# One visit instead of two for the attention's products with v, with two column groups in banks of the first layer's pool

## The chip, the core and the metric

The kernel runs on one core of a Trainium2 chip. Its engines have queues of their own: TensorE (PE, matrix products; PEld is its weight load), VectorE (DVE), ScalarE (ACT), GpSimd (POOL, here the issuer of loads) and SyncE (SP, here the issuer of stores and of transposing transfers). The metric is the device time of one execution, in microseconds. PE writes its results to PSUM, which has eight banks of 512 float32 per partition.

## What is computed

Attention within chunks of 64 rows, then a two-layer network on its output, cut from the reference:

```python
# q, k, v: (8, 8, 576, 64); chunks of 64 rows of the sequence
scores = scale * np.matmul(q_c, k_c.transpose(0, 1, 2, 4, 3))
scores = scores - np.max(scores, axis=-1, keepdims=True)
attn = np.exp(scores)
attn = attn / (np.sum(attn, axis=-1, keepdims=True) + 1e-09)
out = np.matmul(attn, v_c)
# x: (4608, 512) = out with its 8 heads side by side; w_in (512, 2048), w_out (2048, 512)
h = x @ w_in
g = h * (1.0 / (1.0 + np.exp(-beta * h)))
return g @ w_out
```

## The kernel before

The 4608 rows are cut into 18 **units** of 256 rows (four chunks for each of eight heads), and units are paired into nine **blocks** of 512 rows. A unit's attention has five steps. `emit_T` brings q and k into transposed form (from unit 8 on by transposing transfers on SP). `emit_sc` multiplies them: 32 small matmuls (64x64 tiles of the array) into a PSUM tile of two banks, and ACT takes the exponential of it into `et`. `emit_pv` multiplies `et` with v. A column of constants stands beside the 64 columns of v, so that each of the products has 65 columns, the last of which is the sum for the norm. `emit_norm` (DVE) takes the reciprocal of these sums and multiplies, into `x16`. From unit 6 on `emit_xt_dma` (SP) then writes `x16` transposed into `xt`, the first layer's input.

A unit has two **halves** `s` of 128 rows; one half is eight column groups (four `g` for each of two row halves `r` of the array, each `r` with a PSUM bank of its own), and each group is written by two matmuls, one for each 64 partitions `c`. So a half is 16 matmuls.

The first layer of block j (`emit_m`, 16 groups m) is four matmuls of 512 columns into one bank `hps`, then tanh on ACT (`sg`, L326), then the **gate** on DVE (L306), which reads `hps` and `sg` and writes `gt`. The second layer is done with seven products of half size (`emit_prod`, each in two parts t of eight matmuls of 256 columns, L434) on sums of parts of `gt` (`emit_sum`, DVE, L378) and of the weights; their results are gathered in the banks `ya` and `yb`, from which ACT copies or DVE adds (L454) them out, and SP stores them.

PSUM from block 3 on: `ps_p`, a ring of four banks, for the `hps` tiles; `ps_s`, one tile of two banks, for a unit's scores and then for its products with v, first one half, then the other; `ya` and `yb`. A tile of a ring is given out when the readers of its last content are done. Before block 3 a pool `ps_x` has two banks in the place of `ya` and `yb`, and units below 8 put one half there and the other half in `ps_s`, with all 32 matmuls in one visit of PE. A **visit** is a run of such small matmuls between two groups of full size.

The order on every engine is the order in which the program is written: nothing reorders it. In block j the main loop makes a list of items for the first layer of block j, the products of block j-1 and the attention of units 2j+2 and 2j+3, each with a place between 0 and 1, and emits them sorted by place (and by priority, the second number, where places are equal). For a unit from 8 on, with `a0` its start and `w` = 0.43 its share of the block:

```python
return [(a0, 2, ("sc", u)), (a0 + 0.34 * w, 3, ("pv", u, 0)),
        (a0 + 0.35 * w, 3, ("norm", u, 0)), (a0 + 0.60 * w, 3, ("pv", u, 1)),
        (a0 + 0.61 * w, 3, ("norm", u, 1)), (a0 + 0.10 * w, 3, ("T", u + 1))]
```

Units 8 to 17 are worked on in blocks 3 to 7, two in each. The first unit of a block starts at 0.03, the second at 0.46.

Of the kernel before, what the change touches and what calls it, by code (L numbers as in the profile page):

```python
# [8 lines left out]
FP32 = mybir.dt.float32  # L9
FP16 = mybir.dt.float16  # L10
ACTF = mybir.ActivationFunctionType
ALU = mybir.AluOpType
# [3 lines left out]
def kernel(  # L16
# [10 lines left out]
    nc = tc.nc  # L27
    B, H, S, D = q.shape
# [9 lines left out]
    NV = 16  # L38
# [8 lines left out]
    rd_p = ctx.enter_context(tc.tile_pool(name="rd", bufs=2))  # L47
    x_p = ctx.enter_context(tc.tile_pool(name="x16", bufs=4))
# [5 lines left out]
    ps_p = ctx.enter_context(tc.tile_pool(name="ps_p", bufs=4, space=bass.MemoryType.PSUM))  # L54
    ps_s = ctx.enter_context(tc.tile_pool(name="ps_s", bufs=1, space=bass.MemoryType.PSUM))
    ps_x_open = tc.tile_pool(name="ps_x", bufs=1, space=bass.MemoryType.PSUM)
    ps_x = ps_x_open.__enter__()
# [12 lines left out]
    vbig = big.tile([128, NV, H, VP], FP16)  # L70
# [5 lines left out]
    XU = 8  # L76
# [91 lines left out]
    x_t = {}  # L168
    x16_t = {}
# [68 lines left out]

    def emit_pv(u, halves=(0, 1)):
        et = et_t[u]  # L240
        for s in halves:
            i = 2 * u + s
            pool, tag = (ps_x, "x") if s == 0 and u < XU else (ps_s, "s")
            x = pool.tile([128, 2, 4, 128], FP32, tag=tag, name="x")
            for g in range(4):
                for r in range(2):
                    for c in range(2):
                        nc.tensor.matmul(  # L248
                            out=x[64 * c:64 * c + 64, r, g, 0:D + 1],
                            lhsT=(et[64 * r:64 * r + 64, s, 4 * c + g, :] if u < XU else  # L250
                                  et[64 * r:64 * r + 64, g % 2, 4 * s + 2 * c + g // 2, :]),
                            rhs=vbig[64 * r:64 * r + 64, i % NV, 4 * c + g, 0:D + 1],
                        )
            x_t[u, s] = x

    def emit_norm(u, s):
        x = x_t.pop((u, s))
        rd = rd_p.tile([128, 2, 4, 1], FP32, tag="rd", name="rd")
        nc.vector.reciprocal(out=rd, in_=x[:, :, :, D:D + 1])
        x16 = x_p.tile([128, 2, 4, D], FP16, tag="x16", name="x16")  # L260
        for r in ([0, 1] if u < 2 else [slice(0, 2)]):
            o = x16[:, r]
            nc.vector.tensor_tensor(  # L263
                out=o, in0=x[:, r, :, 0:D], in1=rd[:, r].to_broadcast(list(o.shape)), op=ALU.mult
            )
        x16_t[u, s] = x16
# [196 lines left out]
    with tc.manual_schedule():  # L463
# [3 lines left out]
        for a, eng, dst in ((0, nc.sync, raw0), (1, nc.gpsimd, qk0[1])):  # L467
            for i, src in enumerate((q, k)):
                eng.dma_start(
                    out=dst[i],  # L470
                    in_=src[0, HH * a:HH * a + HH, 0:UNIT, :].rearrange("h (p r) d -> p h r d", r=2),
# [27 lines left out]
        loads_to(4)  # L499
        emit_idle(8, 128)  # L500
        emit_pv(0)
        emit_norm(0, 0)
        emit_norm(0, 1)
        emit_idle(12, 128)
        emit_xt_pe(0, 0)
# [4 lines left out]
        emit_m(0, 0, 0, 256)  # L510
        emit_m(0, 1, 0, 256)
        emit_pv(1)
        emit_norm(1, 0)
        emit_norm(1, 1)
        emit_m(0, 2, 0, 256)
# [9 lines left out]
        for s in range(4):  # L525
            for t in range(4):
                if s == 2 and t == 1:
                    emit_T(2)
                    for i in (0, 2, 1, 3):
                        emit_wt(i, (0,))  # L530
                    emit_wt(0, (1,))
                if s == 2 and t == 2:
                    emit_sc(2)
                if s == 3 and t == 0:
                    emit_pv(2)
                    emit_norm(2, 0)
                    emit_norm(2, 1)
                    emit_T(3)
                if s == 3 and t == 3:
                    emit_xt_unit(2)  # L540
                emit_t(0, t, 4 * s, 4 * s + 4)
# [16 lines left out]

        def att_items(u, a0, w):
            if u >= XU:  # L560
                return [(a0, 2, ("sc", u)), (a0 + 0.34 * w, 3, ("pv", u, 0)),
                        (a0 + 0.35 * w, 3, ("norm", u, 0)), (a0 + 0.60 * w, 3, ("pv", u, 1)),
                        (a0 + 0.61 * w, 3, ("norm", u, 1)), (a0 + 0.10 * w, 3, ("T", u + 1))]
            return [(a0, 2, ("sc", u)), (a0 + 0.40 * w, 3, ("pv", u)),
                    (a0 + 0.41 * w, 3, ("norm", u, 0)), (a0 + 0.55 * w, 3, ("norm", u, 1)),
                    (a0 + (0.70 if u + 1 < XU else 0.10) * w, 3, ("T", u + 1))]

        for j in range(1, NB):
# [4 lines left out]
            if j == 1:  # L573
                items += [(0.04 * m, 0, ("h", m)) for m in range(8)]
                items += [(0.32 + 0.085 * (m - 8), 0, ("m", m)) for m in range(8, KFF)]
                items += [(0.30, 3, ("T", 4)), (0.52, 2, ("sc", 4)), (0.70, 2, ("pv", 4)), (0.71, 3, ("norm", 4, 0)),
                          (0.80, 3, ("norm", 4, 1)), (0.56, 3, ("Th", 5, "kT")), (0.63, 3, ("Th", 5, "qT"))]
                items += [(c, 3, ("wt", i)) for i, c in ((1, 0.47),)]
            else:
                m0 = 0.36 if j == 2 else 0.02  # L580
                items += [(m0 + (1 - m0) * m / KFF, 0, ("m", m)) for m in range(KFF)]
                for i, p in enumerate((1, 2, 6, 5, 7, 3, 4)):
                    for t in range(2):
                        items.append((0.98 * (2 * i + t) / 14, 1, ("prod", p, t)))
                if j == NB - 1:
                    for i, c in ((2, 0.74), (0, 0.82), (1, 0.86), (3, 0.90)):
                        items.append((c, 4, ("pre", i)))
                for i in range(4):
                    s0 = (0.01, 0.08, 0.25, 0.33)[i] if j == 2 else 0.005 + 0.07 * i
                    items.append((s0, 4, ("sum", i)))  # L590
                if j == 2:
                    items += [(c, 3, ("wt", i)) for i, c in ((2, 0.36), (3, 0.55))]
                    items += [(0.03, 0, ("sc", 5)), (0.06, 2, ("xp", 4, 0)), (0.09, 2, ("xp", 4, 1)),
                              (0.17, 2, ("pv", 5)), (0.18, 3, ("norm", 5, 0)), (0.19, 3, ("norm", 5, 1)),
                              (0.24, 3, ("T", 6)), (0.30, 2, ("xp", 5, 0)), (0.32, 2, ("xp", 5, 1))]
                if j + 1 < NB:
                    if j == 2:
                        items += att_items(6, 0.36, 0.27) + att_items(7, 0.60, 0.27)
                    else:
                        for i in range(2):  # L600
                            items += att_items(2 * j + 2 + i, 0.03 + 0.43 * i, 0.43)
# [64 lines left out]
```

## Time and profile before

| What | Value |
|---|---|
| Three timed runs | 282.84, 284.44, 285.32 us |
| The profiled execution's own time | 282.25 us |
| Its span, first to last instruction | 280.5 us |
| PE busy | 270.0 us (96%) |
| DVE busy | 194.4 us (69%) |
| ACT busy | 147.6 us (53%) |
| One block, from one to the next product behind the first unit's scores (155.57 to 183.99 us) | 28.42 us |
| of it DVE busy | 20.18 us |
| PE's granted clock in every stretch | 1.00 |

The page cuts the span into 40 slices; a digit is the busy share of an engine in tenths. A line of the timeline has the start, the length of a run of equal instructions, engine, line, operation, what it writes from what, shape and count; in brackets stands the idle time before it and what ended that. Matmuls overlap, so a group's length is longer than what it costs: the cost is read from start to start. The same holds on DVE, where the end of one instruction lies beside the start of the next. A line of the view of waits has who waited for whom, the total in us, the number of waits and the longest.

### The profile page before, as it was taken

The numbers are of one execution on the slowest core, as the hardware profiler recorded it, in microseconds if no ns is written. First come the engines' busy times: TensorE is split into PE (matmuls) and PEld (weight loads), VectorE is DVE, ScalarE is ACT, GpSimd is POOL, SyncE is SP. The second block draws the span as 40 slices with busy tenths as digits, with TensorE's granted clock in tenths as the row PEclk, the third lists the DMA queues.
The fourth block names the chain that finished last, engine by engine and source line by source line (L and its number), as shares of the span: only waits on it lengthen the run. The fifth ranks groups of instructions, "written<-read, shape, count | busy, mean of one in ns | idle before, by whom it ended". The sixth has DMA issues, their size and how long they took to land.

```text
span 280.5 us, 7406 instructions
## 1 busy us (share of the span) xinstructions
PE 270.0 (96%) x3090; PEld 173.4 (62%) x3090; DVE 194.4 (69%) x327; ACT 147.6 (53%) x234; POOL 97.2 (35%) x124
## 2 busy tenths in 40 slices
PE   7689999899999999999999999999999999999995
PEld 3465446757665566666666666666666666666784
DVE  3567464899987588658865885579566956775841
ACT  3278417876564555545554546464645454544521
POOL 8864478499739607060451542000000000000000
PEclk9999999999999999999999999999999999999999
DMA  9999999999999999999899999971847124111213
GB/s 137 168 196 204 187 181 206 217 171 154 174 149 134 189 182 98 149 154 165 85 167 170 148 120 160 173 115 26 127 112 115 22 56 115 37 40 37 75 40 112
DMA packets 145952, 36.92 MB, mean 132 GB/s; under 512 B 130048, under 2 KB 145408, under 8 KB 145920
## 3 DMA queue, kind: packets, MB, share of 16 engines
q0 software_dynamic: 101216, 18.10, 85.6%
q1 hardware_dynamic: 44704, 18.37, 35.1%
q8 instruction: 24, 0.39, 0.6%
q14 instruction: 8, 0.07, 0.1%
HBM read 36.71 MB, written 9.44 MB: 165 GB/s over the span
## 4 chain that ended last, share of the span: by engine, by line
PE 82%; DMA 6%; DVE 5%; POOL 4%; ACT 1%; issue 1%; POOLq 0%
PE hps L318 38%; PE ya L434 17%; PE yb L434 12%; PE acc L434 6%; PE ops L339 4%; DMA qu<-in_q_dram 3%; DMA win<-in_moe_w_in_dram 2%; PE x L248 2%; DVE gt L306 2%; POOL vbig L115 2%; PE sc L214 1%; DVE x L263 1%; PE sc L227 1%; POOL qu L107 1%; ACT sg L326 1%
## 5 line engine op out<-in xcount | busy, mean ns | idle before, releaser
L326 ACT ACTIVATE sg<-hps,bt 128x512 f32<-128x512 f32 (+1 forms) x158 | 101.9, 651 | 93.2 <-PE hps L318 91.5
L318 PE MATMUL hps<-xt,win 128*128 128x512 f16 (+1 forms) x632 | 143.3, 360 | 1.9 <-DMA win<-in_moe_w_in_dram 0.8
L306 DVE SCALAR_TENSOR_TENSOR gt<-sg,hps 128x512 f16<-128x512 f32 (+1 forms) x158 | 99.6, 637 | 61.8 <-ACT sg L326 61.4
L318 PEld LDWEIGHTS <-win 128*128 128x128 f16 x632 | 59.7, 98 | 43.9 <-issue 1.8
L434 PEld LDWEIGHTS <-sm 128*128 128x128 f16 x512 | 49.2, 98 | 15.1
L434 PEld LDWEIGHTS <-gt 128*128 128x128 f16 x384 | 37.0, 98 | 11.9
L101 POOL DMA_DIRECT2D qu<-in_q_dram x22 | 18.6, 856 | 53.6 <-DMA qT<-qu 46.9
L115 POOL DMA_DIRECT2D vbig<-in_v_dram x40 | 34.1, 874 | 8.5 <-DMA wout<-in_moe_w_out_dram 4.3
L434 PE MATMUL ya<-wt,sm 128*128 128x256 f16 x208 | 27.0, 273 | 0.0
L263 DVE TENSOR_TENSOR x<-x,rd 128x512 f16<-128x512 f32 (+1 forms) x40 | 25.2, 637 | 1.2
L378 DVE TENSOR_TENSOR sm<-gt 128x2048 f16<-128x2048 f16 (+1 forms) x17 | 19.7, 1157 | 0.3
L101 POOL DMA_DIRECT2D ku<-in_k_dram x22 | 18.8, 875 | 0.0
L339 PE MATMUL ops<-wout,gt 128*128 128x512 f16 x64 | 14.5, 379 | 0.0
L434 PE MATMUL ya<-wout,gt 128*128 128x256 f16 x104 | 13.5, 273 | 0.0
L434 PE MATMUL yb<-wt,sm 128*128 128x256 f16 x104 | 13.5, 273 | 0.0
L434 PE MATMUL yb<-wout,sm 128*128 128x256 f16 x104 | 13.5, 273 | 0.0
L434 PE MATMUL ya<-wt,gt 128*128 128x256 f16 x104 | 13.5, 273 | 0.0
L434 PE MATMUL yb<-wout,gt 128*128 128x256 f16 x104 | 13.5, 272 | 0.0
L236 ACT ACTIVATE et<-sc 128x1024 f16<-128x1024 f32 (+1 forms) x9 | 7.3, 833 | 11.5 <-PE sc L227 11.5
L248 PEld LDWEIGHTS <-et 64*64 64x64 f16 x576 | 7.2, 106 | 9.2 <-issue 6.1
L451 ACT COPY osb<-ya 128x512 f32<-128x512 f32 x18 | 10.6, 587 | 2.4 <-PE ya L434 2.2
L248 PE MATMUL x<-vbig,et 64*64 64x65 f16 x576 | 10.7, 196 | 0.3 <-DMA vbig<-in_v_dram 0.2
(62 smaller groups left out, 185.0 us busy)
## 6 DMA issues: line engine op xcount, KB each, us to landing
out_dram<-osb SPq DMA_DIRECT2D x32, 256.0 KB, 4.1
vbig<-in_v_dram POOLq DMA_DIRECT2D x32, 128.0 KB, 6.8
qu<-in_q_dram POOLq DMA_DIRECT2D x20, 128.0 KB, 5.5
ku<-in_k_dram POOLq DMA_DIRECT2D x20, 128.0 KB, 6.0
win<-in_moe_w_in_dram POOLq DMA_DIRECT2D x8, 256.0 KB, 8.5
wout<-in_moe_w_out_dram POOLq DMA_DIRECT2D x4, 512.0 KB, 12.9
qu<-in_q_dram POOLq DMA_DIRECT2D x4, 256.0 KB, 7.4
ku<-in_k_dram POOLq DMA_DIRECT2D x4, 256.0 KB, 6.3
```

Source lines behind the costliest of these rows:

```text
L101: nc.gpsimd.dma_start(out=tv[off:off + n, sp], in_=src[b, :, s:s + n, :].rearrange("h p d -> p h d"),)
L115: nc.gpsimd.dma_start(out=vbig[off:off + n, i % NV, :, 0:D], in_=v[b, :, s:s + n, :].rearrange("h p d -> p h d"),)
L236: nc.scalar.activation(out=et[:, s], in_=sc[:, s], func=ACTF.Exp, scale=scale)
L248: nc.tensor.matmul(out=x[64 * c:64 * c + 64, r, g, 0:D + 1], lhsT=(et[64 * r:64 * r + 64, s, 4 * c + g, :] if u < XU else et[64 * r:64 * r ...
L263: nc.vector.tensor_tensor(out=o, in0=x[:, r, :, 0:D], in1=rd[:, r].to_broadcast(list(o.shape)), op=ALU.mult)
L306: nc.vector.scalar_tensor_tensor(out=gt_t[j][:, m, c0:c0 + n], in0=sg[:, 0:n], scalar=1.0, in1=hps[:, 0:n], op0=ALU.add, op1=ALU.mult,)
L318: nc.tensor.matmul(out=hps[:, 0:n], lhsT=w_in16[m // 2][:, kk, (m % 2) * 128:(m % 2) * 128 + 128], rhs=xr[:, c0 // CH:(c0 + n) // CH, 2 * ...
L326: nc.scalar.activation(out=sg[:, 0:n], in_=hps[:, 0:n], func=ACTF.Tanh, scale=bt[:, m:m + 1])
L339: nc.tensor.matmul(out=ops, lhsT=gt_t[j][:, kk, t * 128:(t + 1) * 128], rhs=w_out16[kk // 4][:, kk % 4, :], start=(kk == 0), stop=(kk == K ...
L378: nc.vector.tensor_tensor(out=sm[i][:, lo:hi, :], in0=a, in1=b, op=op)
L434: nc.tensor.matmul(out=dst, lhsT=lhsT, rhs=rhs, start=(p in (1, 2, 5) and kk == 0 and (t == 0 or last)), stop=(kk == 7 and (t == 1 or last ...
L451: nc.scalar.copy(out=o, in_=acc)
```

## The change

From unit 8 on both halves are multiplied in one visit of 32 matmuls. A unit has then 16 column groups (eight n for each of two r) of 65 columns. Seven n fit into one bank (7 x 65 = 455 of 512 columns), so the two-bank tile of `ps_s` takes n = 0 to 6 of both r, packed at a step of 65 columns; n = 7 of both r goes into two banks `xe` taken from `ps_p`, and is written first. The norms are cut anew. The first (`s == 0`) takes the reciprocal and the product of the two extra groups, one column and 64 columns each, then one reciprocal of the other 14 sums and the product for n = 0 to 3 (512 columns). The second is the product for n = 4 to 6 alone (384 columns). `x16` is one tile for both halves. The places in the list become 0.36 w for the visit, 0.361 w and 0.42 w for the norms, instead of 0.34 and 0.60 for the visits and 0.35 and 0.61 for the norms. Units below 8 are as they were.

```diff
     def emit_pv(u, halves=(0, 1)):
         et = et_t[u]
+        if u >= XU:
+            x = ps_s.tile([128, 2, 512], FP32, tag="s", name="x")
+            y = [ps_p.tile([128, 512], FP32, tag="p", name="xe") for _ in range(2)]
+            x_t[u] = (x[:, :, 0:7 * (D + 1)].rearrange("p r (n d) -> p r n d", n=7), y)
+            for n in (7, 0, 1, 2, 3, 4, 5, 6):
+                for r in range(2):
+                    s, g = divmod(n, 4)
+                    i = 2 * u + s
+                    o = x_t[u][0][:, r, n] if n < 7 else y[r][:, 0:D + 1]
+                    for c in range(2):
+                        nc.tensor.matmul(
+                            out=o[64 * c:64 * c + 64],
+                            lhsT=et[64 * r:64 * r + 64, g % 2, 4 * s + 2 * c + g // 2, :],
+                            rhs=vbig[64 * r:64 * r + 64, i % NV, 4 * c + g, 0:D + 1],
+                        )
+            return
...
+    def norm_part(x16, x, rd):
+        nc.vector.tensor_tensor(
+            out=x16, in0=x[:, :, :, 0:D], in1=rd.to_broadcast(list(x16.shape)), op=ALU.mult
+        )
+
+    def emit_norm_whole(u, s):
+        x, y = x_t[u][0:2]
+        if s == 0:
+            rx = rd_p.tile([128, 2, 8, 1], FP32, tag="rx", name="rx")
+            x16 = x_p.tile([128, 2, 2, 4, D], FP16, tag="x32", name="x16", bufs=2)
+            for r in range(2):
+                nc.vector.reciprocal(out=rx[:, r, 7], in_=y[r][:, D:D + 1])
+                nc.vector.tensor_scalar(out=x16[:, 1, r, 3], in0=y[r][:, 0:D], scalar1=rx[:, r, 7], scalar2=None,
+                                        op0=ALU.mult)
+            nc.vector.reciprocal(out=rx[:, :, 0:7], in_=x[:, :, :, D:D + 1])
+            norm_part(x16[:, 0], x[:, :, 0:4], rx[:, :, 0:4])
+            x_t[u] = (x, rx, x16)
+            x16_t[u, 0] = x16[:, 0]
+            return
+        x, rx, x16 = x_t.pop(u)
+        norm_part(x16[:, 1, :, 0:3], x[:, :, 4:7], rx[:, :, 4:7])
+        x16_t[u, 1] = x16[:, 1]
...
-                return [(a0, 2, ("sc", u)), (a0 + 0.34 * w, 3, ("pv", u, 0)),
-                        (a0 + 0.35 * w, 3, ("norm", u, 0)), (a0 + 0.60 * w, 3, ("pv", u, 1)),
-                        (a0 + 0.61 * w, 3, ("norm", u, 1)), (a0 + 0.10 * w, 3, ("T", u + 1))]
+                return [(a0, 2, ("sc", u)), (a0 + 0.36 * w, 3, ("pv", u)),
+                        (a0 + 0.361 * w, 3, ("norm", u, 0)), (a0 + 0.42 * w, 3, ("norm", u, 1)),
+                        (a0 + 0.10 * w, 3, ("T", u + 1))]
```

More of the change, by code (lines that the diff above doesn't have):

```diff
@@ L240, in emit_pv @@
         et = et_t[u]
+        if u >= XU:
[14 more added lines that the diff above has]
+            return
         for s in halves:
             i = 2 * u + s
-            pool, tag = (ps_x, "x") if s == 0 and u < XU else (ps_s, "s")
+            pool, tag = (ps_x, "x") if s == 0 else (ps_s, "s")
             x = pool.tile([128, 2, 4, 128], FP32, tag=tag, name="x")
@@ L249, in emit_pv @@
                             out=x[64 * c:64 * c + 64, r, g, 0:D + 1],
-                            lhsT=(et[64 * r:64 * r + 64, s, 4 * c + g, :] if u < XU else
-                                  et[64 * r:64 * r + 64, g % 2, 4 * s + 2 * c + g // 2, :]),
+                            lhsT=et[64 * r:64 * r + 64, s, 4 * c + g, :],
                             rhs=vbig[64 * r:64 * r + 64, i % NV, 4 * c + g, 0:D + 1],
@@ L254, in emit_pv @@
             x_t[u, s] = x
+    def norm_part(x16, x, rd):
[19 more added lines that the diff above has]
+        x16_t[u, 1] = x16[:, 1]
     def emit_norm(u, s):
+        if u >= XU:
+            emit_norm_whole(u, s)
+            return
         x = x_t.pop((u, s))
```

## The prediction

> **What bounds the kernel now.** I read the page first, then the waits of the matrix engine (PE), then its timeline, then VectorE's (DVE's). The page's span, PE's busy tenths and the chain that ended last:
>
> ```profile
> span 280.5 us, 7406 instructions
> ...
> PE   7689999899999999999999999999999999999995
> ...
> PE 82%; DMA 6%; DVE 5%; POOL 4%; ACT 1%; issue 1%; POOLq 0%
> ```
>
> From the ninth slice on PE is full, and it owns 82% of the chain. A busy PE could still hide gaps, so the view of waits comes second. Cut to 85 to 245 us, it has one line for PE:
>
> ```profile
> PE hps L318 <- DVE gt L306: 0.3, 1, 0.3
> ```
>
> So in the blocks that the change touches (from 98 us on) PE waits for nobody; time is the sum of what PE issues. The two costs to know are those of a visit with 16 matmuls and of one with 32, and PE's timeline has both. Columns: start, length of the merged group, what it is.
>
> ```profile
> 85.99 1.04 PE L434 MATMUL acc<-wout,sm 128*128 128x256 f16 x8
> 86.96 0.45 PE L248 MATMUL x<-vbig,et 64*64 64x65 f16 x32
> 87.33 1.90 PE L318 MATMUL hps<-xt,win 128*128 128x512 f16 x8
> ...
> 158.19 1.03 PE L318 MATMUL hps<-xt,win 128*128 128x512 f16 x4
> 159.14 0.32 PE L248 MATMUL x<-vbig,et 64*64 64x65 f16 x16
> 159.40 1.04 PE L318 MATMUL hps<-xt,win 128*128 128x512 f16 x4
> 160.27 1.04 PE L434 MATMUL yb<-wout,gt 128*128 128x256 f16 x8
> 161.14 1.03 PE L318 MATMUL hps<-xt,win 128*128 128x512 f16 x4
> 162.01 1.04 PE L434 MATMUL ya<-wt,sm 128*128 128x256 f16 x8
> 162.97 0.32 PE L248 MATMUL x<-vbig,et 64*64 64x65 f16 x16
> 163.22 1.04 PE L318 MATMUL hps<-xt,win 128*128 128x512 f16 x4
> ```
>
> Groups overlap in the listing, so costs are read from start to start. A first-layer group (hps, four matmuls of 512 columns) takes 161.14 to 162.01, 0.87 us; a product group (eight of 256 columns) 160.27 to 161.14, 0.87 us. From 158.19 to 159.40 is 1.21 us for one hps group and a visit: the visit costs 0.34. From 162.01 to 163.22, 1.21 again: 0.34. Unit 7 has both halves in one visit already: 85.99 to 87.33 is 1.34, so 32 matmuls cost 0.47 us. Hence 16 more matmuls cost 0.13 and merely entering and leaving about 0.21.
>
> **The change part by part.** *One visit for two (PE).* Ten units (8 to 17) lose two visits of 0.34 and gain one of 32 matmuls of the same shape, 0.47: 0.68 - 0.47 = 0.21 us each, 10 x 0.21 = 2.1 us, all of it on PE's unbroken stream. That the 32 are spread over four banks rather than two isn't shown; the order keeps what the row has (two column halves in turn, then the other row half with a bank of its own). The new visit holds more waits inside (for v, for the second extra bank), but unit 7's held waits on transfers of v in its middle too and still cost 0.47, so satisfied ones are priced at nothing. Bounds for the visit: 0.47 (the row) and 0.68 (as dear as two); I take 0.47.
>
> *The two extra banks (the ring of four).* The hps tiles rotate through four banks; a group may start when the gate on DVE (L306) has read the tile four places back. Two places now go to the extra columns, so the two hps groups behind the visit reuse the tiles of the two groups just before it, not those two places further back. I walked DVE's queue through the first unit of one block. Its rows now:
>
> ```profile
> 158.23 0.69 DVE L306 SCALAR_TENSOR_TENSOR gt<-sg,hps 128x512 f16<-128x512 f32 x1 [0.27 <-ACT sg L326]
> 159.97 0.69 DVE L306 SCALAR_TENSOR_TENSOR gt<-sg,hps 128x512 f16<-128x512 f32 x1 [1.05 <-ACT sg L326]
> 160.58 1.22 DVE L378 TENSOR_TENSOR sm<-gt 128x2048 f16<-128x2048 f16 x1
> 161.71 0.20 DVE L259 RECIPROCAL rd<-x 128x8 f32<-128x8 f32 x1
> 161.94 0.69 DVE L263 TENSOR_TENSOR x<-x,rd 128x512 f16<-128x512 f32 x1
> 162.55 0.68 DVE L306 SCALAR_TENSOR_TENSOR gt<-sg,hps 128x512 f16<-128x512 f32 x1
> 163.15 0.68 DVE L454 TENSOR_TENSOR osb<-yb,osb 128x512 f32<-128x512 f32 x1
> ```
>
> After the change PE runs: hps at 158.19, visit to 159.53, hps at 159.53, product at 160.40, hps at 161.27, product, hps at 163.01. The hps at 159.53 needs the gate that ends at 158.92 (158.23 + 0.69): 0.6 us early. The one at 161.27 needs the gate that ends at 160.66: 0.6 early. These gates stand ahead of the norm on DVE, so the recut norm can't delay them. The hps at 163.01 needs the first extra bank, read after one reciprocal and one small multiply: started at 161.71, they end by about 162.16, 0.85 early. The ring gets tighter, but I price it at nothing; if the cover went, every missing microsecond would land on PE at once. In the block's second unit the tightest is the hps group two behind the visit: about 173.5 against a gate that ends 172.9, 0.6 again.
>
> *The recut norms (DVE).* Two pairs of reciprocal and 512-wide multiply become: two reciprocals of one column, two multiplies of 64 columns, a reciprocal of 14, a multiply of 512 and one of 384. Start to start a reciprocal takes 0.23 (161.71 to 161.94), a 512-wide multiply 0.61 (161.94 to 162.55): now 2 x 0.84 = 1.68 per unit. The 64-wide multiply has no row. Its bounds are the reciprocal's 0.20 and the 256-wide multiply's 0.42; the line through 256 (0.42) and 512 (0.69) gives 0.22, which I take, and 0.56 for 384. So 3 x 0.23 + 2 x 0.22 + 0.61 + 0.47 = 2.2, half a microsecond more per unit. DVE is busy 20.2 of the 28.4 us of a block, and rises to about 21.2: no bound. What matters is that the first piece grows from 0.84 to 1.74 in one go, and what queues behind it: the gate of the next hps (ends 164.1 instead of 163.2; its bank is wanted at 166.5) and the add that frees yb (ends 164.7 instead of 163.8). The next writer of yb is the product at 165.84, which comes at 165.6: 0.9 of margin left of 2.0. With both small multiplies at 0.42 it is 0.5. Price: nothing.
>
> *What moves.* The second norm ends earlier (about 165.1 instead of 166.4), and with it the two-bank tile is free for the next scores and the second transposing transfer of `x16` is issued by SP, in the same place of its queue; the first is issued about 0.9 later (163.4 for 162.6). Both feed the next block, whose first hps stands at 182.66. V of the second half is wanted some 3.5 us sooner, but for unit 8, the first, POOL issues its loads at 64.35 us for a visit at 102.29, and they land within 10.7 us; later loads on POOL wait for the q buffers, not for PE's reading of v. ACT's list is the same.
>
> **A rule against it.** DVE's list grows by three instructions per unit, and the trace has it at 0.5 us. The Trainium skill (VectorE: DVE Perf Modes, "Rules for kernel authors") advises to keep the number of VectorE operations small, as each pays its own drain. And Perfetto Trace Analysis ("Optimization Strategy") says that the same gap coming back on the engine that should be full can mean too few PSUM buffers for the next tile. By these the change would trade PE's gain for a bubble behind each visit; by the margins above it doesn't, and the trace decides for those.
>
> **Sum.** 2.1 us, from the profiled execution's 282.25 us (span 280.5): 280.1. That execution lies below all three timed runs (282.84 to 285.32), whose median is 284.44; taken from the median it is 282.3, which I forecast. It is 0.75% faster; about 1% is what a measurement of this kernel can tell from no change.
>
> **Rivals.** *Full gain* (the forecast), 0.78. For it: a measured 32-matmul visit, no PE waits, four margins above 0.5.
>
> *The visit costs more than 0.47*, because four banks and waits after the first matmuls break the overlap. At 0.58, half way to 0.68, the gain is 1.0: 283.4. At 0.68 the change doesn't do what it says: 284.4. Against: unit 7's visit. 0.15.
>
> *The ring starves PE* (the slower one). Place: the two hps groups behind each visit, held by gates (ACT's tanh, then DVE) only two groups back. The trace has the like once: at 91.31 us PE waited 0.34 for a gate behind a norm and an add. It decides from 0.21 us of waiting per unit, that is, if the gates came 0.7 us later than in the walk. At 0.34 for both groups of ten units it is 6.8 - 2.1 = 4.7 slower: 289.1; at one per unit 1.3 slower, 285.7. Against: the margin of 0.6 before gates that the norm can't delay. 0.07.
>
> **Numbers.** With the runs' spread of some 1.2 us to either side of their median, the forecast alone spans 281 to 283.5. Reaching down to the sum from the profiled execution and up past the visit that gains nothing gives 280.1 to 284.7; the starved ring is left out. The full gain sits 0.25% short of the 1% line, so the spread takes it across in over a quarter of its cases: faster 0.22. Slower by over 1% needs 2.8 us, the upper half of the ring's case: 0.05. Within 1%: 0.73.
>
> **What would show it.** Right: in PE's timeline ten groups of 32 with 0.47 from the neighbours' starts, blocks of 28.0 instead of 28.4 us, and no PE wait after 98 us. Wrong: a line of PE waiting on DVE's gates, adds or the small multiplies (ring, or yb), a visit of 0.5 or more, or small multiplies of 0.4 and up. Wrong altogether if PE is held by something that no wait shows now.

## The result, and the profile after

The changed kernel took 280.64 us (median of six runs, 280.26 to 282.10) against 283.95 us of the kernel before, beside which it ran: a ratio of 0.9896 with a 95% interval of 0.9858 to 0.9934. Faster, then, by 0.7 to 1.4%, where 0.75% was forecast; 280.64 lies inside the range of 280.1 to 284.7. A second comparison on one chip gave 280.73 against 282.70 us, 0.9938 (0.9917 to 0.9960).

The page of the changed kernel (profiled execution 281.67 us): span, PE's busy tenths, its granted clock, and the chain that ended last.

```profile
span 279.9 us, 7409 instructions
...
PE   7589999899999999999999999999999999999995
...
PEclk9959999999999999999999999999999999999999
...
PE 84%; DVE 6%; POOL 3%; DMA 2%; ACT 2%; issue 1%; DVEq 0%; ACTq 0%; POOLq 0%
```

The span is only 0.6 us shorter than before, which would be a puzzle if the row of the clock were not there: in the third slice (14 to 21 us) PE was granted about half its clock. That is in the **head**, the stretch before the blocks run full, which the change does not touch. So the two profiles are compared from the first place that it does: unit 8's scores start at 98.34 us before and at 100.05 us after, and from there to the end it is 280.5 - 98.34 = 182.16 us before and 279.9 - 100.05 = 179.85 us after. The touched stretch is 2.31 us shorter. The repeats' profiles say the same: 182.16 and 179.88 us. The line that opens the stretch, in the kernel before and in the changed one:

```profile
98.34 0.44 PE L214 MATMUL sc<-qT,kT 64*64 64x64 f16 x32
```

```profile
100.05 0.45 PE L214 MATMUL sc<-qT,kT 64*64 64x64 f16 x32
```

PE's waits of the changed kernel between 85 and 245 us (who waited for whom, total us, times, longest) are the one that was there before, in block 2, ahead of the change:

```profile
PE hps L359 <- DVE gt L347: 0.3, 1, 0.3
```

PE's timeline around the first visit of the block whose scores start at 155.98 us (start, length, what):

```profile
158.98 1.03 PE L359 MATMUL hps<-xt,win 128*128 128x512 f16 x4
159.93 0.23 PE L251 MATMUL xe<-vbig,et 64*64 64x65 f16 x4
159.99 0.39 PE L251 MATMUL x<-vbig,et 64*64 64x65 f16 x28
160.31 1.04 PE L359 MATMUL hps<-xt,win 128*128 128x512 f16 x4
161.19 1.04 PE L475 MATMUL yb<-wout,gt 128*128 128x256 f16 x8
162.06 1.03 PE L359 MATMUL hps<-xt,win 128*128 128x512 f16 x4
162.92 1.04 PE L475 MATMUL ya<-wt,sm 128*128 128x256 f16 x8
163.80 1.03 PE L359 MATMUL hps<-xt,win 128*128 128x512 f16 x4
```

From 158.98 to 160.31 is 1.33 us for one hps group (0.87) and the visit: 0.46. The place of the second visit, 162.92 to 163.80, is now a bare product group of 0.88. A block takes 27.97 us (128.39 to 156.36) instead of 28.42. DVE in the same block:

```profile
159.02 0.69 DVE L347 SCALAR_TENSOR_TENSOR gt<-sg,hps 128x512 f16<-128x512 f32 x1 [0.28 <-ACT sg L367]
160.76 0.69 DVE L347 SCALAR_TENSOR_TENSOR gt<-sg,hps 128x512 f16<-128x512 f32 x1 [1.05 <-ACT sg L367]
161.37 1.22 DVE L419 TENSOR_TENSOR sm<-gt 128x2048 f16<-128x2048 f16 x1
162.50 0.16 DVE L282 RECIPROCAL rx<-xe 128x1 f32<-128x1 f32 x1
162.70 0.28 DVE L283 TENSOR_SCALAR x<-xe,rx 128x64 f16<-128x64 f32 x1
162.90 0.16 DVE L282 RECIPROCAL rx<-xe 128x1 f32<-128x1 f32 x1
163.09 0.28 DVE L283 TENSOR_SCALAR x<-xe,rx 128x64 f16<-128x64 f32 x1
163.29 0.23 DVE L285 RECIPROCAL rx<-x 128x14 f32<-128x14 f32 x1
163.56 0.69 DVE L272 TENSOR_TENSOR x<-x,rx 128x512 f16<-128x512 f32 x1
164.17 0.68 DVE L347 SCALAR_TENSOR_TENSOR gt<-sg,hps 128x512 f16<-128x512 f32 x1
164.76 0.68 DVE L495 TENSOR_TENSOR osb<-yb,osb 128x512 f32<-128x512 f32 x1
```

The margins can be read off these two listings. The hps at 160.31 wanted the gate that ends at 159.02 + 0.69 = 159.71 (0.6 us early), the one at 162.06 the gate that ends at 161.45 (0.6), the one at 163.80 the small multiply that ends at 162.98 (0.8), and yb's next writer, at 166.40, the add that ends at 165.44 (0.96).

### The profile page after: what moved, and what is told of

The parts are those of the page before. It is cut to its first block, busy times and chain, and to the rows that moved or that the text cites. A ratio compares the mean times of both kernels' runs of the same rounds, so it can differ in the third digit from the quotient of the medians.

```text
span 279.9 us, 7409 instructions
## 1 busy us (share of the span) xinstructions
PE 269.3 (96%) x3090; PEld 174.4 (62%) x3090; DVE 197.9 (71%) x357; ACT 147.7 (53%) x234; POOL 97.0 (35%) x124
## 4 chain that ended last, share of the span: by engine, by line
PE 84%; DVE 6%; POOL 3%; DMA 2%; ACT 2%; issue 1%; DVEq 0%; ACTq 0%; POOLq 0%
PE hps L359 40%; PE ya L475 17%; PE yb L475 12%; PE acc L475 6%; PE ops L380 5%; DVE gt L347 3%; DMA win<-in_moe_w_in_dram 2%; PE sc L214 1%; POOL vbig L115 1%; PE sc L227 1%; ACT sg L367 1%; PE xp L320 1%; PE x L251 1%; DVE x L304 1%; DVE kT L159 1%
## 5 line engine op out<-in xcount | busy, mean ns | idle before, releaser
L367 ACT ACTIVATE sg<-hps,bt 128x512 f32<-128x512 f32 (+1 forms) x158 | 101.8, 650 | 92.5 <-PE hps L359 76.9
L359 PE MATMUL hps<-xt,win 128*128 128x512 f16 (+1 forms) x632 | 145.4, 366 | 1.6 <-DMA win<-in_moe_w_in_dram 0.9
L359 PEld LDWEIGHTS <-win 128*128 128x128 f16 x632 | 61.4, 99 | 44.2 <-issue 1.4
L475 PEld LDWEIGHTS <-gt 128*128 128x128 f16 x384 | 36.9, 98 | 12.0
L272 DVE TENSOR_TENSOR x<-x,rx 128x512 f16<-128x512 f32 (+1 forms) x20 | 12.4, 620 | 0.3
L304 DVE TENSOR_TENSOR x<-x,rd 128x512 f16<-128x512 f32 (+1 forms) x20 | 11.3, 583 | 0.6
L380 PEld LDWEIGHTS <-gt 128*128 128x128 f16 x64 | 6.0, 98 | 6.9
```

The costliest lines, as they stand in the source:

```text
L272: nc.vector.tensor_tensor(out=x16, in0=x[:, :, :, 0:D], in1=rd.to_broadcast(list(x16.shape)), op=ALU.mult)
L304: nc.vector.tensor_tensor(out=o, in0=x[:, r, :, 0:D], in1=rd[:, r].to_broadcast(list(o.shape)), op=ALU.mult)
L359: nc.tensor.matmul(out=hps[:, 0:n], lhsT=w_in16[m // 2][:, kk, (m % 2) * 128:(m % 2) * 128 + 128], rhs=xr[:, c0 // CH:(c0 + n) // CH, 2 * ...
L367: nc.scalar.activation(out=sg[:, 0:n], in_=hps[:, 0:n], func=ACTF.Tanh, scale=bt[:, m:m + 1])
L380: nc.tensor.matmul(out=ops, lhsT=gt_t[j][:, kk, t * 128:(t + 1) * 128], rhs=w_out16[kk // 4][:, kk % 4, :], start=(kk == 0), stop=(kk == K ...
L475: nc.tensor.matmul(out=dst, lhsT=lhsT, rhs=rhs, start=(p in (1, 2, 5) and kk == 0 and (t == 0 or last)), stop=(kk == 7 and (t == 1 or last ...
```

## Experiments

Theory: a visit of PE costs some 0.21 us for entering and leaving, and having ten of them less is the whole gain. Rivals: the gain comes from the layout, the norms or their places; it is really larger, 3 us, as the first comparison's medians have it; or the ring of four banks takes part of it back.

### Both kernels again, for the clock of the head

Both are run without an edit.

> The kernel before, unchanged. It is here for the granted clock of its own runs: the changed kernel's runs lay at 280.26 to 282.10 us, with 280.26 to 280.74 where the mean clock was 0.994 or 0.999 and 281.67 and 282.10 where it was 0.988. Theory (the head's clock scatters whatever the kernel, the change saves 2.3 us): this kernel's runs show mean clocks between 0.985 and 1.000, and at equal clock lie some 2.3 us above the changed kernel's. Rival (the change gains over 3 us): at equal clock the difference is 3 us or more. Blocks in the profile 28.43 us.

> The changed kernel, unchanged, for a narrower interval. Theory (2.3 us of 282.3 on the stretch that the change touches): ratio 0.992, 0.989 to 0.994. Rival (a real gain of the median's 3.3 us): ratio 0.988. Blocks in the profile 27.97 us in both.

Measured in one comparison, on one chip: 282.99 us for the kernel before (ratio to itself 1.001, 0.9991 to 1.0029) and 280.73 for the changed one. Sorted by each run's mean granted clock, with the number of runs:

| Mean clock | Before, median us | Changed, median us |
|---|---|---|
| 0.999 to 1.000 | 282.49 (13) | 280.44 (2) |
| 0.991 to 0.994 | 282.78 (16) | 280.93 (3) |
| 0.988 | 283.92 (6) | 282.37 (1) |

The kernel before scatters in the same way, so that scatter is not the change's doing, and at equal clock the difference is 1.6 to 2.1 us, not 3.3. The rival of 3 us falls; that the classes come out a little under 2.3 rests on six runs of the changed kernel. Blocks were 28.42 us (100.34 to 128.76 between scores) and 27.97 (98.72 to 126.69). The profile of this kernel before has its scores of unit 8 at 100.34 and a span of 282.5 us: 182.16 from there to the end, as in the first.

### Two visits of 16 with the changed layout

The loop over n becomes a function of its own, called once for n = 7, 0, 1, 2 and, as the second visit, for n = 3 to 6.

```diff
-            for n in (7, 0, 1, 2, 3, 4, 5, 6):
+            emit_pv_part(u, (7, 0, 1, 2))
...
-                return [(a0, 2, ("sc", u)), (a0 + 0.36 * w, 3, ("pv", u)),
-                        (a0 + 0.361 * w, 3, ("norm", u, 0)), (a0 + 0.42 * w, 3, ("norm", u, 1)),
+                return [(a0, 2, ("sc", u)), (a0 + 0.36 * w, 3, ("pv", u, 0)),
+                        (a0 + 0.406 * w, 3, ("pv", u, 1)),
+                        (a0 + 0.407 * w, 3, ("norm", u, 0)), (a0 + 0.445 * w, 3, ("norm", u, 1)),
```

> The changed kernel's banks and recut norms, but the 32 matmuls in two visits of 16 with one group of full size between them; the norms follow the second visit. Theory (each visit costs 0.21 us to enter and leave, and that alone is the gain): ten visits more, 2.1 to 2.3 us slower than the changed kernel, blocks 28.4 us, ratio to the kernel before 1.000. Rival (the gain comes from the layout, the recut norms or their places): blocks stay near 28.0, ratio 0.992.

Measured: 283.47 us, ratio 1.0024 (1.0009 to 1.0038); 2.7 us slower than the changed kernel beside it. PE's timeline:

```profile
131.15 1.03 PE L367 MATMUL hps<-xt,win 128*128 128x512 f16 x4
132.10 0.22 PE L248 MATMUL xe<-vbig,et 64*64 64x65 f16 x4
132.16 0.27 PE L248 MATMUL x<-vbig,et 64*64 64x65 f16 x12
132.36 1.04 PE L367 MATMUL hps<-xt,win 128*128 128x512 f16 x4
133.32 0.32 PE L248 MATMUL x<-vbig,et 64*64 64x65 f16 x16
133.58 1.05 PE L483 MATMUL yb<-wout,gt 128*128 128x256 f16 x8
```

The first visit costs 132.36 - 131.15 - 0.87 = 0.34 us, the second 133.58 - 132.36 - 0.87 = 0.35: four banks and packed columns cost nothing, and two visits cost what they did. Blocks without a wait are 28.42 us again (185.31 to 213.73 between scores). What is left stands in two waits: from unit 8's scores to the end its profile takes 282.2 - 98.98 = 183.2 us, 3.4 more than the changed kernel's, and two of its blocks are 0.75 and 0.32 us longer than 28.42. The profile puts the first wait (0.6 us, ahead of unit 10's scores) down to a gate that ended at 127.19 us, but a transposing transfer of `xt` landed at about the same time (issued at 122.0, 5.1 us to landing), so which of them it was isn't shown; the second (0.2) is for a transfer. Without the two the run has just the 2.3 us of the ten visits. The layout, the norms and the banks by themselves gain nothing.

### An almost empty visit

```diff
+    def emit_empty(u):
+        t = ps_s.tile([128, 2, 512], FP32, tag="s", name="empty")
+        et = et_t[u]
+        for r in range(2):
+            for c in range(2):
+                nc.tensor.matmul(
+                    out=t[64 * c:64 * c + 64, r, 0:D + 1],
+                    lhsT=et[64 * r:64 * r + 64, 0, 2 * c, :],
+                    rhs=vbig[64 * r:64 * r + 64, 2 * u % NV, 4 * c, 0:D + 1],
+                )
...
+                        (a0 + 0.70 * w, 3, ("empty", u)),
```

> The changed kernel plus one visit per unit from 8 on that holds only four small matmuls (64x65) into the free two-bank tile, which nobody reads. Theory (entering and leaving costs 0.21 us whatever stands inside, 16 matmuls 0.13): 0.21 + 0.03 = 0.24 us per unit, blocks 28.45, 2.4 us slower than the changed kernel, ratio to the kernel before 1.000. Rival (a visit's cost lies in its matmuls, 0.34 / 16 each): 0.085 per unit, blocks 28.14, 0.9 us slower than the changed kernel.

Measured: 289.56 us, ratio 1.025 (1.023 to 1.027), 8.8 us more than the changed kernel: both expectations missed. PE's waits show most of it, 5.7 us:

```profile
PE empty L276 <- DVE x L283: 5.7, 5, 1.1
```

In a block's first unit the added visit stood ahead of the end of the second norm, which still read the two-bank tile, and PE stood for 1.1 us, five times. So this run prices a badly placed visit, not an empty one. In the next one the visit stands behind the norm (0.90 instead of 0.70 in the edit):

> The changed kernel plus one visit of four small matmuls per unit, as in the run with the empty visit, but behind the end of the second norm, so that its two-bank tile is free (there the visit of a block's first unit waited 1.1 us for it). Theory (0.21 us to enter and leave, 16 matmuls 0.13): 0.24 us per unit, blocks 28.45 us, 283.0 us in all. Rival (a visit's cost lies in its matmuls, 0.34 / 16 each): 0.085 per unit, blocks 28.14, 281.4 us.

Measured: 282.87 us, ratio 0.999 (0.9968 to 1.0012): the gain is given back. PE's timeline:

```profile
136.66 1.03 PE L370 MATMUL hps<-xt,win 128*128 128x512 f16 x4
137.62 0.22 PE L276 MATMUL empty<-vbig,et 64*64 64x65 f16 x4
137.78 1.05 PE L486 MATMUL yb<-wt,sm 128*128 128x256 f16 x8
```

From 136.66 to 137.78 is 1.12: the four matmuls cost 0.25 us, and a block is 28.48 (127.11 to 155.59 between scores), 0.51 longer than the changed kernel's. By the price per matmul it would have been 0.17 longer. A visit costs 0.25 with 4 matmuls, 0.34 with 16, 0.47 with 32: about 0.21 plus 8 ns each.

What in the entering and leaving takes the 0.21 us is not separated by any run here. The timeline of the weight loads (PEld) in the kernel before shows one thing that stops there: between groups of full size the first weights are loaded 0.1 to 0.2 us ahead of the first matmul (at 160.06 us for the group at 160.27), but at both ends of a visit only as the matmul starts (159.14 for the visit at 159.14, 159.39 for the group at 159.40). That this is the cause is not shown.

### The extra banks read late

The lines that read the two extra groups are moved from the first norm to the head of the second:

```diff
         if s == 0:
...
-            for r in range(2):
-                nc.vector.reciprocal(out=rx[:, r, 7], in_=y[r][:, D:D + 1])
-                nc.vector.tensor_scalar(out=x16[:, 1, r, 3], in0=y[r][:, 0:D], scalar1=rx[:, r, 7], scalar2=None,
-                                        op0=ALU.mult)
...
-        x, rx, x16 = x_t.pop(u)
+        x, rx, x16, y = x_t.pop(u)
+        for r in range(2):
+            nc.vector.reciprocal(out=rx[:, r, 7], in_=y[r][:, D:D + 1])
+            nc.vector.tensor_scalar(out=x16[:, 1, r, 3], in0=y[r][:, 0:D], scalar1=rx[:, r, 7], scalar2=None,
+                                    op0=ALU.mult)
```

> The changed kernel with the two extra column groups normalised in the second norm instead of the first, so that their banks come back to the ring later; the matmuls and the sum of the work are the same. Theory (the ring's margin is what the early reading buys): in a block's first unit the third hps group behind the visit finds its bank read only about 1.25 us after PE wants it, in the second unit 0.1 to 0.2 us; 1.4 us per block, five blocks, 7 us: blocks 29.4 us, 287.5 us in all, slower than the kernel before, with a line of PE waiting for the small multiplies. Rival (the ring has room, PE is bound by its own work alone): blocks stay at 27.97 and the time at 280.6.

Measured: 282.23 us, ratio 0.9972 (0.9948 to 0.9996), 0.9 us below the kernel before of the same comparison where the change itself brings 2.3: some 1.5 us are lost, not 7. PE waits once in a block, for 0.15 us, and not for the small multiplies. PE's timeline, then DVE's:

```profile
134.84 1.04 PE L475 MATMUL ya<-wt,sm 128*128 128x256 f16 x8
136.03 1.02 PE L359 MATMUL hps<-xt,win 128*128 128x512 f16 x4 [0.15 <-DVE gt L347]
```

```profile
135.30 0.68 DVE L347 SCALAR_TENSOR_TENSOR gt<-sg,hps 128x512 f16<-128x512 f32 x1
135.89 0.68 DVE L495 TENSOR_TENSOR osb<-yb,osb 128x512 f32<-128x512 f32 x1
136.49 0.16 DVE L288 RECIPROCAL rx<-xe 128x1 f32<-128x1 f32 x1
136.69 0.28 DVE L289 TENSOR_SCALAR x<-xe,rx 128x64 f16<-128x64 f32 x1
```

The third hps group behind the visit starts at 136.03, as the gate of the group two places back ends (135.98), while its supposed bank is read until 136.97. So the ring does not turn in a fixed order: while the extra banks are held, the hps groups take turns in the two others, and the price is how late a gate two groups back is. The walk through a ring in fixed turn was wrong for this kernel. And the wait costs more than its line: from 134.84 to 136.03 is 0.32 us more than a product group's 0.87, twice the 0.15 shown. The line counts from the listed end of the group ahead (134.84 + 1.04 = 135.88), while groups that don't wait start 0.17 us before that end (1.04 - 0.87). Five such stops are 1.6 us, the loss that was measured (blocks of 28.28 us, 128.27 to 156.55).

### The last wait of PE

```diff
-                    (a0 + 0.41 * w, 3, ("norm", u, 0)), (a0 + 0.55 * w, 3, ("norm", u, 1)),
+                    (a0 + 0.41 * w, 3, ("norm", u, 0)), (a0 + (0.63 if u == 7 else 0.55) * w, 3, ("norm", u, 1)),
```

> The changed kernel with unit 7's second norm behind the next gate and add on DVE, for the one wait of PE that is left after 60 us (0.34 us for a gate, in block 2). Theory: the wait goes, nothing else moves, 0.3 us faster than the changed kernel, 280.3 us; its own blocks stay at 27.97. Rival: the bank or the transfer that the later norm delays is late next, and the 0.3 us stay or grow.

Measured: 282.75 us, ratio 0.9975 (0.9952 to 0.9998), 0.4 us below the kernel before, so that 2 us of the change's gain are lost. The wait for the gate is gone, and its place is taken (PE's waits from 85 to 255 us):

```profile
PE hps L359 <- DMA xt<-x: 2.0, 1, 2.0
```

The later norm issues unit 7's last transposing transfer at 94.13 us (at 92.4 in the changed kernel), it lands 6.9 us later, and block 3's first hps group, which would have come at 98.9, starts at 101.08. The rival was right: a wait of 0.3 us went, and one of 2 us for a transfer came in its place. The stop costs more than itself, too. Behind it PE was granted 0.50 of its clock from 101.8 to 105.2 us, and from that hps group to unit 8's visit it took 6.46 us (101.08 to 107.54) instead of 4.91 (99.09 to 104.00 in the changed kernel). From unit 7's visit to the end this profile is 3.2 us longer than the changed kernel's: 2.2 for the stop and 1.5 for the clock, less 0.5 for the gate that is no longer waited for. Other executions need not have lost the clock there: the two of twelve with a mean clock of 0.999 or 1.000 took 281.57 and 281.89 us.

### The head's pauses filled

Idle matmuls are products of a tile of zeros that nobody reads. Both kernels have some in the head already; this edit adds 26.

```diff
         emit_T(1)
+        emit_idle(16, 128)
         emit_sc(1, True)
...
         emit_norm(1, 1)
+        emit_idle(10, 128)
```

> The changed kernel with 26 more idle matmuls of 128 columns in PE's pauses between 10 and 17 us. Theory (pauses of PE in the head let the granted clock fall to half for some us in some runs, and that is most of the spread between runs): mean clocks of 0.999 and 1.000 in all runs, times within 0.3 us of 280.4. Rival (the clock falls for another reason, or the idle matmuls stand in the way): mean clocks scatter as before from 0.988 to 0.999, or the times rise by what the idle matmuls take, up to 1.4 us.

Measured: 280.46 us (280.19 to 280.93), mean clocks 0.998 to 1.000 in all six runs, ratio 0.9895 (0.9866 to 0.9923). Without the added ones the changed kernel's clocks went from 0.988 to 0.999 and its times over 2 us. With the same edit on both kernels, in one comparison:

> The kernel before with the 26 idle matmuls in the head's pauses, as the run of the changed kernel with them had, so that the clock of the head is the same in both. Theory (the change saves 10 x 0.23 us in its own stretch and nothing else): clocks of 0.998 and over, 282.7 us, that is 2.3 us above the changed kernel with the same idle matmuls (280.4). Rival (part of the first comparison's 3.3 us belongs to the change): 283.4 us or more.

> The changed kernel with the 26 idle matmuls once more, on the same chip as the kernel before with them. Theory: 280.4 us, spread under 1 us, 2.3 us below the other. Rival: 3 us or more below it.

Measured: 282.82 us (282.50 to 283.88) and 280.45 us (279.75 to 280.67). The difference is 2.37 us, with clocks of 0.999 and 1.000 in every run of both. The kernel before gained nothing from them in the median: 282.76 us without them in the same comparison, ratio 0.9996 (0.9976 to 1.0017). Stretches of the changed kernel without and with the added idle matmuls, each line with the stretch, its length, busy us of PE, PEld, DVE, ACT, POOL, then PE's granted clock, the transfers' share and GB/s:

```profile
10.00:17.00 7.00, 4.10 (x120) 2.96 (x120) 3.95 (x11) 3.29 (x8) 5.72 (x9) 0.84 1.74 185
17.00:24.00 7.00, 7.00 (x48) 5.49 (x47) 4.29 (x12) 5.15 (x11) 3.16 (x5) 0.67 1.43 198
```

```profile
10.00:17.00 7.00, 4.78 (x141) 4.03 (x142) 3.07 (x8) 3.19 (x8) 5.40 (x8) 1.00 1.73 184
17.00:24.00 7.00, 6.56 (x55) 4.89 (x54) 5.55 (x15) 5.68 (x13) 3.64 (x6) 1.00 1.44 198
```

In the first PE is idle for 2.9 of 7 us and is granted 0.84 and then 0.67 of its clock; in the second it is idle for 2.2 us and keeps 1.00. The changed kernel with the added idle matmuls has the lowest medians here, 280.45 and 280.46 us in its two comparisons, but the 0.2 to 0.3 us to those without them are less than its runs' spread.

## Why the prediction was right

*What bounds it:* right. PE's stream is unbroken from block 3 on in both kernels, so every 0.01 us of a visit is on the path, and the touched stretch became shorter by just what the visits lost.

*The visit:* right in mechanism and nearly in size. 0.34 + 0.34 - 0.47 = 0.21 us per unit was forecast; blocks give (28.42 - 27.97) / 2 = 0.23, and 2.31 us in all instead of 2.1. Rounding is the likely reason, not a shown one: the costs were read to 0.01 us from single groups, and ten units multiply it; the difference of whole blocks is the better reading where there is one. The price of the row that was already there, unit 7's visit, carried over to four banks unchanged (0.46 and 0.47).

*The ring and yb:* right for this kernel. Forecast margins 0.6, 0.6, 0.85 and 0.9 us, found 0.6, 0.6, 0.8 and 0.96. The reason behind them was half wrong: the banks are not given out in fixed turn, as the run with the late reading showed, and where they run short PE waits for a gate, not for the extra bank. That a missing microsecond lands on PE "at once" was too kind: a wait shown as 0.15 cost 0.32. The rival of the starved ring was priced too low by the same error: the wait at 91.31 us that it took at 0.34 cost 0.50 (from the hps group at 89.94 to the one at 91.31, less 0.87). That gate (90.58 us) also stood behind a norm alone; the add came after it.

*The norms:* the 64-wide multiply took 0.28 us where 0.22 was taken (bounds 0.20 and 0.42), the one-column reciprocal 0.16 where 0.20 was; start to start the first norm took 164.17 - 162.50 = 1.67 against 1.74. DVE is busy 20.84 us in a block, 0.66 more than before.

*The rule against it:* the Trainium skill's advice against more VectorE operations (VectorE: DVE Perf Modes, "Rules for kernel authors") named a real cost, 0.66 us per block, which lies in DVE's idle time. Its remark on a gap that keeps coming back (Perfetto Trace Analysis, "Optimization Strategy") came true only in the run with the late reading: the same 0.15 us in every block, from too few free banks.

*The total:* the median came out at 280.64, 1.7 us below the forecast, though the saving was right to 0.2 us. Most of the miss is the base it was taken from: the three runs shown had a median of 284.44, six had 283.95, and the 23 runs of the second comparison had 282.70. The profiled execution's 282.25, at full clock, was the better base: minus 2.1 it gives 280.1, and the changed kernel at full clock ran at 280.3 to 280.7. Whether the first runs of the kernel before had a slower head isn't recorded with them. That the first ratio, 0.9896, lies past the 1% line, to which the forecast gave 0.22, was luck of these runs as far as the others show: the second comparison has 0.9938, and the two kernels with the added idle matmuls are 0.8% apart.

## What to carry to other kernels

Where PE is full, count the changes between small-tile and full-size work, not only the matmuls: each visit cost about 0.21 us before its first matmul counted, with 4, 16 or 32 of them in it, and merging two visits gained just that. Price a merge from a merged row if the kernel has one, and then walk each buffer that the merge holds longer, with the time at which its next user comes; margins of 0.6 us were enough here, and moving a reading behind four more DVE instructions used one up. Waits of 0.15 and 0.34 us in the listing cost PE some 0.17 us more than they showed, and one of 2 us in block 3 was followed by 3.4 us at half clock. Before a saving under 1% is read from medians, look at the stretch of the profile that the change touches, and at the granted clock in the rest.

## What was not expected of the hardware

A good part of the spread between runs of one kernel goes with PE's clock. In all six profiles in which it fell it did so in the head, and in one of them once more, behind a stop in block 3. Mean clocks cluster at 0.988, 0.992 to 0.994 and 1.000; at half clock for a time t in a span of 280 us the mean is 1 - t / 560, so these are some 6.7, 3.4 to 4.5 and 0 us at half clock. The median of the kernel before was 283.92 us at 0.988 and 282.49 at full clock. It isn't all of the spread: at 0.998 and over that kernel's runs still lay between 281.92 and 284.97 us, and with the added idle matmuls between 282.50 and 283.88. The Trainium skill (TensorE: Matmul & The Clock Gate, "Part 1: The HAM clock gate") says that PE's clock is halved after an idle window of about 3.4 us that runs free of the kernel's start; steps of about 3.4 us and a granted 0.50 at 17.0 to 20.4 us in the changed kernel's profile agree with it. But no pause of PE in that profile before 17 us was longer than 1.2 us, and a repeat's profile, with PE idle for 3.2 of the 7 us from 10 to 17, kept the full clock; and in the run with unit 7's later norm a stop of 2.05 us was followed by half clock. So an idle time of 3.4 us is not needed, and the pauses alone don't decide it; that the place of the window in time does would fit, but no run here shows it. What is shown is that filling two pauses kept the clock up: it was 0.998 or more in all 18 runs with the added idle matmuls in one comparison and in six in another, and without them in 4 of the changed kernel's 12 and 30 of 81 of the kernel before whose clock is recorded.
